# Regrouping a fused attention and FFN kernel, with weights and v cast in transfers that GpSimd issues

## The chip, the core and the metric

The kernel runs on one core of a Trainium2 chip. The core has TensorE (PE, with its own row PEld for weight loads), VectorE (DVE), ScalarE (ACT), GpSimd (POOL) and SyncE (SP), which work through queues of their own and wait for each other by semaphores; 16 DMA engines move data between HBM and SBUF. The metric is the device time of one execution in microseconds. Before the change the median of three runs was 226.99 us (226.62 to 227.18).

## The reference

Two layers follow each other. The first is a decayed linear attention over 4 batches, 8 heads, 768 positions of 64 elements, in blocks; the second is a bilinear FFN over the 3072 tokens that result.

```
for each block of 64 positions, per batch and head:
    intra = ((qb @ kb.T) * Dmask) @ vb          # Dmask[i,j] = lam**(i-j) for i >= j
    inter = (qb * lam**(pos+1)) @ kv_state
    out   = intra + inter
    kv_state = lam**64 * kv_state + (kb * lam**(63-pos)).T @ vb
x = out, heads side by side: 3072 x 512
y = ((x @ w_a) * (x @ w_b)) @ w_out             # w_a, w_b: 512 x 1536, w_out: 1536 x 512
```

Inputs and output are float32.

## The kernel before

A unit is 128 positions of one batch with all eight heads, so there are 24 units, six to a batch. Units are gathered into groups, and a group passes through the FFN together: `GROUPS` on line 28 is (4, 1, 2, 4, 4, 4, 4, 1). The first four units are packed and treated by code of their own (from line 868), because their q and k come in by eight transfers laid out for them.

**Attention of a unit, in pieces.** `prep_k` scales k and q by powers of lam into one bf16 tile (`make_ks`, `make_qs`, line 401) and, for units in `DMA_T`, issues a DMA transpose on SP; other units are transposed on PE (`piece_T`, `tps`, line 443, with a copy on ACT). `prep_v` casts v from float32 to bf16 on the engine that `VB_ENG` names (`make_vb`, lines 418 and 420). `piece_S` does the scores (`kq`, line 457) and the causal mask: either DVE multiplies PSUM by the triangle `lotri` (line 480) or ACT copies the scores to SBUF first (line 471) and DVE multiplies there (line 472). `piece_V` updates the running state `kvd` in PSUM and copies it to SBUF as `st` (lines 527, 558, 560). `pieces_O` makes the outputs of a pair of units (`o_ps`, line 497), whose evacuation (`evac_o`, lines 520 and 522) writes `xT`, the transposed input of the FFN.

**The FFN in three forms.** `ffn` is the plain form: per slice of 128 columns of d_ff, four matmuls for `a_ps`, four for `b_ps` (line 596), a copy of a on ACT (line 605), a product on DVE (line 623) into `ab`, and later output matmuls `op` (line 643). `ffn_z` replaces the eight block products of a 2 x 2 block matrix product by seven, for w_a and w_b: sums of weight blocks `wz_a`, `wz_b` (`weight_sum`) and of blocks of `xT` (`z_add`, `z_sub`, `z_mix` in `x_sums`, lines 705 to 707) are made beforehand; the partial products go through the PSUM banks U, V and W (line 730), copies of intermediate states on ACT (`snap`, line 811), subtractions on DVE (`oab`, lines 759 to 776) and a product on DVE (`ab`, line 738). The output step `op` has a seven-product form too: `ab_sum` makes sums of `ab` blocks (`zab`, lines 825 to 831), `out_sum` sums of w_out (`wy`, line 290), and `out_half` does half of one of the seven products (line 852). `Z_GROUPS` names the groups that use seven products in the first step (3 to 6), `ZO_GROUPS` those that use them in the output step (4 to 6); group 3 ends in `out_plain` (line 792), groups 0, 1, 2 and 7 are plain in both. A four-unit group needs 168 matmuls of 256 columns in the first step in seven-product form, and 84 of 256 columns in the output step, where the plain output step needs 48 of 512.

**Order.** The order of the work is written out by hand. `PLAN` lists for each group what is to be issued at which slot of its FFN: pieces of attention for coming groups, output halves of the group before (`H`), sums (`SM`, `WS`, `WO`, `X`), casts (`C`). `hook(slot)` issues them at that place, and each engine then takes its instructions in that order, waiting only for their inputs and buffers. Where output halves of the group before stand between the first-step products of a group, the code calls the group joined.

**Loads.** All loads of q, k, v and the weights are issued by SP as plain transfers of float32 (`load_x`, line 187; `load_w`, lines 221 and 228). Weights go into staging slots borrowed from other tiles and are cast to bf16 by DVE, ACT or POOL (`cast_w`, lines 240 to 254); `pump` issues the next pending load when a slot is free or when a unit has come close enough (`LOOKAHEAD`). The output is stored by SP, the very last part by ACT.

Of the kernel before, what the change touches and what calls it, by code (L numbers as in the profile page):

```python
# [22 lines left out]
def _bc(ap, dims):  # L23
# [4 lines left out]
GROUPS = (4, 1, 2, 4, 4, 4, 4, 1)  # L28
# [3 lines left out]
LOOKAHEAD = {9: 2, 10: 1}  # L32
DMA_T = range(7, 24)
KEEP_GROUPS = 2
PACK = 4

PLAN = {
# [38 lines left out]
}  # L81
Z_GROUPS = (3, 4, 5, 6)
ZO_GROUPS = (4, 5, 6)
FIN_AT = 5
N_LATE = 3
EV_ENG = {(u, b): "act" for u in range(24) for b in range(2)}
# [992 lines left out]
```

## Time and profile before

| | |
|---|---|
| median of three runs | 226.99 us |
| span of the profiled execution | 224.66 us (224.7 on the page) |
| granted TensorE clock | 1.000 |
| PE, DVE, ACT, POOL busy | 214.6, 164.8, 123.2, 101.1 us |
| HBM read, written | 28.32 MB, 6.29 MB |
| first matmul of the FFN | 18.16 us |
| first seven-product matmul | 84.74 us |
| last matmul group starts | 218.92 us |

The profiled execution has no other time than its span beside it: the time of the runs also holds what lies around the first and last instruction, and median and span are 2.33 us apart. Busy spans of one engine can overlap by some tens of nanoseconds, so counts times mean durations give more than the busy time, and for PE the distance between the starts of neighbouring rows says what an instruction costs. A line such as L596 is one line of the kernel, and several uses can share it. The window view gives, for each stretch, busy microseconds and the number of instructions of each engine, the granted clock, the mean busy share of the DMA engines and the GB/s that they moved.

### The profile page before, as it was taken

The page shows a single profiled execution, that of the slowest core. Times are in us where ns is not written, and L with a number is a line of the kernel's source. Part 1 is how long each engine was busy: PE and PEld are TensorE (multiplying, and loading weights), DVE is VectorE, ACT ScalarE, POOL GpSimd, SP SyncE. Part 2 cuts the span into 40 slices and gives each one's busy share as a digit, 9 for nine tenths or more (in the row PEclk, how much of TensorE's full clock was granted, in tenths as well). Part 3 has the DMA queues.
Part 4 walks back from the last instruction along what each step waited for, and adds up shares of the span by engine and source line. Part 5 has one row for each costly group of instructions (what it writes and reads, how often), then busy time and mean ns, then how long its engine had stood idle before and what let it go on. Part 6 is the DMA issues. An engine that isn't in the chain of part 4 may idle for free.

```text
span 224.7 us, 5609 instructions
## 1 busy us (share of the span) xinstructions
PE 214.6 (96%) x2235; PEld 158.8 (71%) x2235; DVE 164.8 (73%) x269; ACT 123.2 (55%) x251; POOL 101.1 (45%) x95
## 2 busy tenths in 40 slices
PE   7699999989989999999999999899999999999994
PEld 2375444437768757887547878688888888887994
DVE  1895673599699659989878999968686765777440
ACT  3586446017544247775366988776536665533322
POOL 6061004256895075541459359786417722052000
PEclk9999999999999999999999999999999999999999
DMA  4999999998999999999999999652021100112042
GB/s 137 316 231 356 356 384 346 276 217 192 229 198 218 219 180 240 204 253 247 175 240 243 243 206 202 138 98 48 2 88 55 50 1 4 47 48 95 0 143 93
DMA packets 99081, 39.42 MB, mean 175 GB/s; under 512 B 85488, under 2 KB 95088, under 8 KB 99056
## 3 DMA queue, kind: packets, MB, share of 16 engines
q1 hardware_dynamic: 98768, 39.00, 78.0%
q8 instruction: 17, 0.28, 0.5%
q10 hardware_dynamic: 288, 0.07, 0.1%
q14 instruction: 8, 0.07, 0.1%
HBM read 28.32 MB, written 6.29 MB: 154 GB/s over the span
## 4 chain that ended last, share of the span: by engine, by line
PE 80%; DVE 6%; DMA 6%; ACT 3%; issue 2%; SPq 1%; ACTq 0%; DVEq 0%
PE U L730 17%; PE op L852 12%; PE b_ps L596 9%; PE op L643 8%; PE V L730 8%; PE a_ps L596 8%; PE op L792 5%; PE W L730 4%; DMA wst<-in_moe_w_b_dram 4%; PE o_ps L497 3%; DMA k<-in_k_dram 3%; PE kq L457 2%; PE kvd L527 1%; SPq L350 1%; DVE m L480 1%
## 5 line engine op out<-in xcount | busy, mean ns | idle before, releaser
L811 ACT COPY u<-U 128x512 f32<-128x512 f32 x48 | 28.4, 591 | 16.9 <-PE U L730 16.6
L401 POOL TENSOR_TENSOR qk<-kf,lp_k 128x512 bf16<-128x512 f32 x18 | 19.8, 1099 | 34.6 <-DMA kf<-in_k_dram 23.1
L623 DVE TENSOR_TENSOR ab<-a_sb,b_ps 128x128 bf16<-128x128 bf16 (+2 forms) x48 | 19.2, 417 | 14.0 <-ACT a_sb L605 11.1
L480 DVE TENSOR_TENSOR m<-kq,lotri 128x512 bf16<-128x512 f32 x40 | 25.7, 684 | 3.8 <-PE kq L457 3.6
L596 PE MATMUL a_ps<-xT,wa_sb 128*128 128x128 bf16 (+2 forms) x200 | 27.8, 268 | 0.6 <-ACT xT L520 0.5
L596 PE MATMUL b_ps<-xT,wb_sb 128*128 128x128 bf16 (+2 forms) x192 | 27.5, 272 | 0.7 <-ACT oab L736 0.5
L738 DVE TENSOR_TENSOR ab<-oab 128x1024 bf16<-128x1024 bf16 x24 | 18.4, 767 | 10.5 <-ACT oab L736 10.5
L401 POOL TENSOR_TENSOR qk<-qf,lp_q 128x512 bf16<-128x512 f32 x20 | 25.2, 1259 | 1.2 <-DMA qf<-in_q_dram 1.2
L605 ACT CAST a_sb<-a_ps 128x128 bf16<-128x128 f32 (+2 forms) x48 | 17.1, 375 | 14.4 <-PE a_ps L596 14.3
L643 PE MATMUL op<-wo_sb,ab 128*128 128x512 bf16 (+2 forms) x120 | 22.8, 337 | 0.2 <-DVE wo_sb L254 0.2
L596 PEld LDWEIGHTS <-wa_sb 128*128 128x128 bf16 x200 | 16.6, 98 | 6.6 <-issue 0.7
L596 PEld LDWEIGHTS <-wb_sb 128*128 128x128 bf16 x192 | 15.7, 98 | 7.3 <-DVE wb_sb L251 0.7
L730 PEld LDWEIGHTS <-wz_a 128*128 128x128 bf16 x192 | 18.2, 98 | 3.6 <-issue 0.7
L730 PEld LDWEIGHTS <-wz_b 128*128 128x128 bf16 x192 | 18.7, 98 | 2.2
L730 PE MATMUL U<-xT,wz_a 128*128 128x256 bf16 x96 | 18.3, 272 | 0.0
L730 PE MATMUL U<-xT,wz_b 128*128 128x256 bf16 x96 | 18.3, 272 | 0.0
L520 ACT CAST xT<-o_ps 128x512 bf16<-128x512 f32 (+1 forms) x24 | 12.2, 556 | 10.7 <-PE o_ps L497 10.5
L420 POOL CAST vb<-vf 128x512 bf16<-128x512 f32 x14 | 10.9, 778 | 13.9 <-DMA vf<-in_v_dram 13.9
L769 DVE TENSOR_TENSOR oab<-U,u 128x512 bf16<-128x512 f32 x24 | 16.4, 682 | 0.4 <-PE U L730 0.4
L730 PEld LDWEIGHTS <-wa_sb 128*128 128x128 bf16 x144 | 13.4, 97 | 4.5 <-issue 1.7
L643 PEld LDWEIGHTS <-ab 128*128 128x128 bf16 x120 | 10.1, 98 | 8.6 <-issue 0.3
L736 ACT CAST oab<-U 128x512 bf16<-128x512 f32 x24 | 14.2, 591 | 3.6 <-PE U L730 3.5
(126 smaller groups left out, 453.8 us busy)
## 6 DMA issues: line engine op xcount, KB each, us to landing
vf<-in_v_dram SPq DMA_DIRECT2D x24, 256.0 KB, 4.8
qf<-in_q_dram SPq DMA_DIRECT2D x20, 256.0 KB, 4.6
kf<-in_k_dram SPq DMA_DIRECT2D x20, 256.0 KB, 4.6
out_dram<-o_sb SPq DMA_DIRECT2D x18, 256.0 KB, 2.5
wst<-in_moe_w_a_dram SPq DMA_DIRECT2D x6, 512.0 KB, 8.5
wst<-in_moe_w_b_dram SPq DMA_DIRECT2D x6, 512.0 KB, 9.0
wst<-in_moe_w_out_dram SPq DMA_DIRECT2D x6, 512.0 KB, 10.6
out_dram<-o_kept SPq DMA_DIRECT2D x5, 256.0 KB, 4.4
```

The lines of the kernel that those rows point to most:

```text
L401: eng_of(eng).tensor_mul(dst.rearrange("p (c b) d -> p b c d", b=2), x[:].rearrange("p (b c) d -> p b c d", b=2), lp.rearrange("p (b c) o ...
L480: nc.vector.tensor_mul(m, kq[i], lotri_bc)
L596: nc.tensor.matmul(ps[:, lo:hi], lhsT=w_sb[:, s, f * 128:(f + 1) * 128], rhs=xT[:, s, lo:hi], start=(s == 0), stop=(s == KS - 1), skip_gro ...
L605: nc.scalar.copy(a_sb[:, :gt], ps[:, :gt])
L623: nc.vector.tensor_mul(ab[:, f, :gt], a_sb[:, :gt], ps[:, :gt])
L643: nc.tensor.matmul(op[:, lo:hi], lhsT=ab[:, f, t * 128:(t + 1) * 128], rhs=wo_sb[:, f, lo:hi], start=(f == 0), stop=(f == FC - 1))
L730: nc.tensor.matmul(ps[:, k, :], lhsT=wt[:, s, n * 128:(n + 1) * 128], rhs=rhs[i][:, s, :], start=(fresh and k == 0 and s == 0), stop=True, ...
L736: nc.scalar.copy(oab[:, 0], U)
L738: nc.vector.tensor_mul(ab[:].rearrange("p (h i) (t c) -> p h i t c", h=2, t=2)[:, :, n], o5[:, :, :, 0, :], o5[:, :, :, 1, :])
L769: nc.vector.tensor_sub(oab[:, 1], U, v1)
L811: nc.scalar.copy(t, ps)
L852: nc.tensor.matmul(ps[:, t, :], lhsT=lhs[p][:, n, t * 128:(t + 1) * 128], rhs=rhs[:, n, :], start=fresh, stop=True, skip_group_check=True)
```

## The change

`GROUPS` becomes (4, 2, 4, 4, 4, 4, 2). Group 0 and the two-unit group 1 are plain; groups 2 to 6 use seven products in both steps, the last one with blocks of 128 instead of 256 columns of `xT`. `out_plain` and the special end of the last plain group go away. v and the weights are loaded by transfers that GpSimd issues and that write bf16 straight into the tiles that the matmuls read (v into a pool of eight buffers), so the staging slots and all casts go away. Each such transfer has a place in `PLAN` (`L`), the first eleven entries a list of their own (`HEAD_L`), headed by a one-element copy on POOL that waits for the first chunk of k. SP keeps the loads of q and k; three of the pairs (units 4 to 6) are held by one-element memsets on DVE until their place in the plan. PE transposes the units 4 to 9, DMA the units 10 to 23. Masks are written into one tile for both halves, in place where ACT copies the scores; where ACT copies both, one DVE instruction of 1024 elements masks them. The whole plan and the tables that give work to engines are new.

```
-GROUPS = (4, 1, 2, 4, 4, 4, 4, 1)
+GROUPS = (4, 2, 4, 4, 4, 4, 2)
-DMA_T = range(7, 24)
+DMA_T = (10, 11, 12, 13, 14, 15, 16, 17, 18, 19, 20, 21, 22, 23)
+HEAD_L = (('gate', ('k', 0)), ('v', 0), ('v', 1), ('v', 2), ('v', 3), ('a', 0), ('a', 1), ('b', 0), ('b', 1),
+  ('a', 2), ('b', 2))
+N_VB = 8
 PLAN = {
     0: [
+        (2, 'L', ('a', 3)), (3, 'L', ('b', 3)), (5, 'L', ('a', 4)), (6, 'L', ('a', 5)), (7, 'L', ('b', 4)),
+        (9, 'L', ('b', 5)), (10, 'L', ('o', 0)), (11, 'L', ('qk', 4)), (12, 'L', ('o', 1)),
...
+JOINED = (3, 4, 5, 6)
-Z_GROUPS = (3, 4, 5, 6)
-ZO_GROUPS = (4, 5, 6)
+Z_GROUPS = (2, 3, 4, 5, 6)
...
+        if w == "v":
+            t = prep_pool.tile([128, H, D], BF16, name="vb", tag="vb", bufs=N_VB)
+            nc.gpsimd.dma_start(out=t, in_=vr[b, nb])
         else:
             t = ld_pool.tile([128, H, D], F32, name=w + "f", tag=w + "f")
+            if gate:
+                nc.vector.memset(t[0:1, 0, 0:1], 0.0)
+            nc.sync.dma_start(out=t, in_={"q": qr, "k": kr}[w][b, nb])
...
         if kind == "o":
+            nc.gpsimd.dma_start(out=wo_sb[:, 2 * c:2 * c + 2, :], in_=wo_r[:, 2 * c:2 * c + 2, :])
         else:
+            w, r = (wa_sb, wa_r) if kind == "a" else (wb_sb, wb_r)
+            nc.gpsimd.dma_start(out=w_part(w, c), in_=w_part(r, c))
...
+    def load(x):
+        kind, i = x
+        if kind == "gate":
+            nc.gpsimd.tensor_copy(tiny, x4[i[0], i[1]][0:1, 0, 0, 0:1])
+        elif kind == "qk":
+            for w in "kq":
+                load_x(w, i, True)
+        elif kind == "v":
+            load_x("v", i)
+        else:
+            load_w(kind, i)
...
+    def mask(kq, n_act=0):
+        m = msk_pool.tile([128, H, 128], BF16, name="m", tag="m")
+        ms = [m[:, :HP], m[:, HP:]]
+        if n_act == 2:
+            for i in range(2):
+                nc.scalar.copy(ms[i], kq[i])
+            nc.vector.tensor_mul(m, m, lotri_all)
+            return ms
...
-        if g not in ZO_GROUPS:
-            out_plain(u0, ab, hook)
-        elif own:
+        if own:
             fin.pop()()
-            for i in range(14):
-                hook(3 * NP + i)
+            for i in range(3 * NP, 3 * NP + 16):
+                hook(i)
```

More of the change, by code (lines that the diff above doesn't have):

```diff
@@ new lines @@
+Z_GROUPS = (2, 3, 4, 5, 6)
+KEEP = 4
+EV_ENG = {(4, 0): 'act',
+  (4, 1): 'dve',
+  (5, 1): 'dve',
+  (6, 0): 'act',
+  (6, 1): 'dve',
+  (8, 1): 'dve',
+  (10, 0): 'act',
+  (10, 1): 'dve',
+  (11, 0): 'act',
+  (12, 0): 'dve',
+  (14, 1): 'dve',
+  (15, 0): 'dve',
+  (15, 1): 'dve',
+  (19, 1): 'dve',
+  (22, 1): 'act'}
+MASK_ACT = {4: 1,
+  5: 0,
+  6: 2,
+  7: 1,
+  8: 0,
+  9: 2,
+  10: 1,
+  11: 0,
+  12: 1,
+  13: 1,
+  14: 2,
+  15: 1,
+  16: 0,
+  17: 1,
+  18: 0,
+  19: 1,
+  20: 1,
+  21: 0,
+  22: 1,
+  23: 0}
@@ new lines @@
+KV_ENG = {3: 'dve',
+  4: 'act',
+  5: 'act',
+  6: 'dve',
+  7: 'act',
+  8: 'act',
+  9: 'dve',
+  10: 'dve',
+  11: 'dve',
+  12: 'act',
+  13: 'act',
+  14: 'act',
+  15: 'act',
+  16: 'dve',
+  17: 'dve',
+  18: 'act',
+  19: 'act',
+  20: 'act',
+  21: 'act',
+  22: 'act',
+  23: 'act'}
+PQ_ENG = {4: 'pool',
+  5: 'pool',
+  6: 'pool',
+  7: 'pool',
+  8: 'dve',
+  9: 'pool',
+  10: 'pool',
+  11: 'dve',
+  13: 'pool',
+  14: 'dve',
+  15: 'pool',
+  17: 'pool',
+  20: 'pool',
+  21: 'pool',
+  22: 'pool',
+  23: 'dve'}
@@ new lines, in ffn, with ffn_plain @@
+        ops = [ps_bank("op", [128, d_model], F32, hold=True) for _ in range(n)]
+        for c in range(FC // 2):
+            for t in range(n):
+                out_mms(ops[t], ab, t, range(2 * c, 2 * c + 2))
+                if c == FC // 2 - 1:
+                    store(u0 + t, ops[t], 0, d_model)
+                hook(slot)
+                slot += 1
+        bank["held"].clear()
+    def ffn_plain(u0, n, xT, hook):
+        gt = n * BLK
+        ab = ab_pool.tile([128, FC, 512], BF16, name="ab", tag="ab")
@@ L870 @@
     xs4 = {"q": scr[0][:, 0:4, :], "k": scr[1][:, 0:4, :]}
+    for x in HEAD_L:
+        load(x)
     xT4 = {"q": scr[0][:, 4:8, :], "k": scr[1][:, 4:8, :]}
@@ L945 @@
     scale4("k", 1, 1)
-    for u in range(n0 - 1):
-        make_vb(u, "pool")
     scores4(0, (0, 1), ((5, 6), (0, 1)))
@@ L983 @@
     inter(3)
-    cast_w("a", 0, "first")
     evac_o((2, 3), 0)
```

478 lines of the change are left out of this document (189 added, 289 removed), and 90 rows, old and new, of the table PLAN.

## The prediction

> **What bounds the kernel now.** I read the page's busy shares first, then the windows by stage, then the timeline of the matmuls for their pitch and for the holes between them.
>
> ```profile
> PE 214.6 (96%) x2235; PEld 158.8 (71%) x2235; DVE 164.8 (73%) x269; ACT 123.2 (55%) x251; POOL 101.1 (45%) x95
> ```
>
> PE has work nearly always, so a microsecond is gained either by fewer matmul columns or by closing a hole. The timeline of PE gives both: when rows follow without a wait, the distance of their starts is the true price, because the busy spans overlap.
>
> ```profile
> 18.16 2.06 PE L596 MATMUL a_ps<-xT,wa_sb 128*128 128x256 bf16 x16
> 22.14 3.63 PE L596 MATMUL b_ps<-xT,wb_sb 128*128 128x512 bf16 x16 [0.20 <-DVE wb_sb L251]
> 29.06 1.89 PE L596 MATMUL a_ps<-xT,wa_sb 128*128 128x512 bf16 x8
> 30.79 1.89 PE L596 MATMUL b_ps<-xT,wb_sb 128*128 128x512 bf16 x8
> 45.94 0.40 PE L443 MATMUL tps<-ident,qk 128*128 128x128 bf16 x4 [0.73 <-DVE qk L401]
> 57.66 0.39 PE L596 MATMUL a_ps<-xT,wa_sb 128*128 128x128 bf16 x4
> 57.88 0.39 PE L596 MATMUL b_ps<-xT,wb_sb 128*128 128x128 bf16 x4
> 64.33 0.86 PE L596 MATMUL a_ps<-xT,wa_sb 128*128 128x256 bf16 x4 [0.46 <-ACT xT L520]
> 74.00 0.60 PE L596 MATMUL b_ps<-xT,wb_sb 128*128 128x256 bf16 x4
> 74.44 0.60 PE L596 MATMUL a_ps<-xT,wa_sb 128*128 128x256 bf16 x4
> 143.09 0.38 PE L730 MATMUL U<-z_sub,wa_sb 128*128 128x256 bf16 x2 [0.81 <-DVE oab L769]
> 204.62 0.38 PE L596 MATMUL b_ps<-xT,wb_sb 128*128 128x128 bf16 x4 [0.49 <-ACT oab L736]
> ```
>
> Pitches: 512 columns 1.73/8 = 0.216 us, 256 columns 0.44/4 = 0.109 (0.11 rounded up), 128 columns 0.22/4 = 0.056. Holes: a chunk of b weights arrives late (22.14), transposes wait for a scaled k (45.94), the two-unit group waits for xT (64.33), and DVE is behind in the seven-product stages (143.09).
>
> The windows say how near DVE is to being the bound there, and how fast weights arrive (columns: PE, PEld, DVE, ACT, POOL busy, clock, DMA share, GB/s):
>
> ```profile
> 11.20:16.80 5.60, 5.42 (x110) 4.28 (x109) 5.53 (x10) 4.80 (x11) 3.50 (x5) 1.00 0.93 230
> 22.40:33.70 11.30, 11.30 (x54) 5.12 (x53) 8.09 (x14) 5.41 (x9) 0.00 (x0) 1.00 1.07 370
> 85.00:105.00 20.00, 19.67 (x211) 16.41 (x209) 18.60 (x31) 14.30 (x27) 8.66 (x9) 1.00 1.26 239
> 119.00:143.00 24.00, 23.21 (x279) 18.63 (x277) 22.32 (x35) 19.97 (x40) 16.47 (x13) 1.00 1.06 204
> 143.00:172.00 29.00, 28.76 (x335) 24.26 (x335) 22.07 (x35) 18.38 (x38) 17.39 (x12) 1.00 0.33 77
> ```
>
> DVE is 93% busy in the first step of both four-unit groups without a neighbour's output step (85 to 105, 119 to 143), 76% where output products of the group before are mixed in. The granted clock is 1.00 throughout and plays no part.
>
> **The sum's base.** The profiled span is 224.66 us, the median 226.99; the terms below are taken off the span and the distance of 2.33 is kept.
>
> **1. Matmul columns.** From the two instruction orders: 512-wide output matmuls 132 to 72, -60 x 0.216 = -13.0; 256-wide output matmuls 264 to 378, +114 x 0.109 = +12.4; 128-wide ones in the FFN's first step 192 to 168 and in the last output 24 to none, against 24 more PE transposes (three units fewer are transposed by DMA): -24 x 0.056 = -1.3. Sum -1.9 us. Seven products instead of eight save only this, since three of the last five groups already had them; little here is open, for these are counts times pitches.
>
> **2. Weights and v.** Removed: 24 v loads and 18 weight loads from SP, their casts on DVE (6 v at 0.81, 12 weight pieces, 12 us in all), ACT (4 v at 0.63, 5 pieces, 7.3 us) and POOL (14 v at 0.78, 5 pieces, 15 us). Added: 42 transfers issued by POOL, the first behind a one-element copy that waits for the first k chunk, which had landed by 8.34 (its scaling started then). Every POOL instruction queues behind these issues: the q and k scalings and the sums.
> The trace has no transfer issued by POOL. SP's issues bound the price: 0.5 us each where free, 1.68 where the four v loads held it (6.71 us for four, from 5.28). I take 1.0, an estimate between them nearer the free rows, since the moment of blocking was one. The 16th issue (the last b chunk) then falls at 8.3 + 16 = 24.3. Data: at the 230 GB/s of the window in which v moved, 1 MB of v needs 4.6 us, from about 10 to 14.5; a 512 KB chunk at 370 GB/s 1.42 us. So the third chunk (first of b) lands near 18.8 and the twelfth near 31.5. PE wants them at 21.4 and 35.2 (its present starts less the gain here). Both hold. Gain: the a stage of 16 x 0.109 + 8 x 0.216 = 3.5 us ended at 22.14 instead of 21.6, -0.5; the first a weights passed casts on POOL and DVE for which PE's weight loads waited 0.4, -0.3; the third v's cast on POOL ended near 15.1, when the state matmuls that use it began, -0.2. I take -1.0; ends -1.5 (some of the waits for k gone too) and, at 1.68 an issue, +2 (last issue 35.2, landing some 2 us after).
> SP keeps the q and k loads, the stores and fourteen DMA transposes instead of seventeen; these no longer stand behind 42 other entries, some of which held the queue for over 4 us (a k load at 31.85). I book nothing for it, since PE's holes name no load of q or k after 11 us. The loads of units 4 to 6 now wait for one-element memsets on DVE, six at no more than the 0.27 of the only memset row; the casts that leave the window 22 to 34 (8.09 of 11.3 busy) cover them, and without that cover they are 1.6 us of DVE.
> Later v loads must wait for one of eight buffers; POOL then holds scalings behind them. 42 issues are 42 us on POOL, whose arithmetic falls from 101 to about 77 (14 k scalings x 1.10, 16 q x 1.26, the sums at 1.64, three weight sums x 3.09): 119 of 222 us, so no bound.
>
> [...]
>
> **3. Holes between 40 and 86 us.** At 44.82 to 46.54 eight transposes (0.45 us of work) took 1.7, 1.3 lost; 63.2 to 65.0 lost 0.9 (evacuation of xT, then the a copy); 85.4 to 86.1 lost 0.5 (z_add). The new order puts 24 output matmuls ahead of the first transposes and six (1.3 us) plus eight transposes between the evacuation and the next FFN group; z sums have 18 output matmuls (3.9 us) as cover, and need 0.7 + 1.3. The k scaling that came late was behind a cast, two weight sums and the state copy on DVE. I take -2.5; ends -2.7 and -1.3, since unit 5's q scaling now follows a 3.09 us weight sum, another scaling and a v issue on POOL, which leaves under a microsecond.
>
> **4. The seven-product stages.** DVE gains 12 us (by means: 24 small `ab` -6.8, casts -12.3, and +18 narrow and 6 narrow `oab`/`ab` about 10, `xT` 6 x 0.68, scalings 8 x 0.69, sums and `o_sb` 11, z sums 2.9; 0.92 of it is net, as busy 164.8 is of the 179 that counts times means give), so 177 of 222. What matters is the third group: PE has 168 x 0.109 = 18.4 plus 3.2 of attention, 21.6; DVE has 18 `oab` x 0.684, 5 `ab` x 0.767, eight mask pieces 5.8, state, scalings, xT 4.0, in all 26.0, net 24. That is over PE by 2.4; before the ratio was 0.93. A lag of about a microsecond fits into the banks: +1.5. The next group: DVE 30.3, PE 31: +0.3. Against it the holes of 143.09 (1.0) and at 121 and 132 (0.4) are in groups that now have 28 against 31: -1.2. Sum +0.6; ends -1.4 and +3.
>
> **5. The last group.** Two units at half width. Per pair PE has 28 x 0.056 = 1.6 us, ACT four copies of 0.37, DVE four of about 0.42; with fourteen output halves of the group before between them this fits. The last pair has none: copy, subtraction and copy on one bank, then copy 0.37, product 0.42, sums before the output products, one on POOL at about 0.8. I count 1.2 of waits against the 0.7 that goes at 204.62: +0.5; ends -0.5 and +2.5. The end: the last copy is 0.37 instead of 0.27 and 128 KB land in 1.7 instead of 1.6: +0.2.
>
> Sum: -1.9 - 1.0 - 2.5 + 0.6 + 0.5 + 0.2 = -4.1, a span of 220.6 and a time of **222.9 us**.
>
> **Rivals.** A: the casting transfers run slower than plain ones, or their issue starves. Place: the first group's weights. At the 230 GB/s that short v rows had, a chunk takes 2.28 us, and the twelfth lands at 14.5 + 27.4 = 41.9 against 35.2: 6.7 late. Without term 2 the rest is -3.1, so 230.6. It decides from a chunk time of (35.2 + 3.1 - 14.5)/12 = 2.0 us, 265 GB/s. For it: v's rate, and no row of such a transfer; against it: the present 370 leaves 3.7 us of slack. [...]
> B: DVE becomes the bound. The third and fourth group need 54.3 of DVE; if no more than 0.95 of the time can be filled, 57.2 against PE's 52.6, +4.6 instead of +0.6 net: 226.9. For it: 22.32 of 24 at 119 to 143, with holes; against it: at 85 to 105 the same ratio cost 0.8.
> C: nearly every hole goes: term 4 at -1.0, term 5 at -0.5, term 2 at -1.5: 220.3 or below.
>
> **Chances.** Forecast 0.50 (221.3 to 225.5), C 0.17, B 0.13, A 0.15, other mishaps 0.05. What a measurement can tell from no change is about 0.3%, 0.7 us. Faster: 0.50 + 0.17 + 0.05 of B = 0.72; same 0.04 (B); slower 0.24. The range of 219.0 to 229.0 leaves out most of A and the best of C.
>
> **What would show it.** Right: b_ps starts before 21.7 and the last b step before 35.5 without a DMA wait; no wait at the first transposes; DVE over 23 us in the third group with PE holes of 1 to 2 us; some 1 us of PE waits in the last pair. Wrong: PE waiting for weights from the transfers, POOL issues far over 1 us with scalings late behind them, or PE losing over 3 us to DVE.

## The result, and the profile after

The changed kernel took 248.47 us (248.11 to 248.74, four runs), the kernel before 227.09 beside it: 1.094 times as long, 95% interval 1.091 to 1.097. The prediction was 222.9 in a range of 219.0 to 229.0, so it was wrong in sign and far out of range. The profiled execution of the changed kernel took 248.11, with a span of 246.4.

The page of the changed kernel, busy time and share of each engine, and the granted clock in 40 slices:

```profile
PE 218.8 (89%) x2262; PEld 164.1 (67%) x2269; DVE 178.4 (72%) x290; ACT 124.7 (51%) x250; POOL 108.8 (44%) x112
...
PEclk9999999959999999997999999999999999999999
```

PE is busy 89% of the span instead of 96%, and the clock, at full speed throughout before, now falls in some slices. DVE and POOL are no busier in share than before (72 and 44% against 73 and 45%). So the loss is in waits of PE. The waits of PE, summed by what ended them (engine, line waited for, total, times, longest):

```profile
PE tps L528 <- POOL qk L498: 4.0, 1, 4.0
PE kq L542 <- DMA qkT<-qk: 3.5, 3, 1.7
PE U L809 <- DVE oab L847: 2.7, 1, 2.7
PE op L907 <- DVE zab L884: 2.4, 1, 2.4
PE b_ps L678 <- DVE ab L705: 1.8, 2, 1.6
```

Before, PE waited 0.8 us for `oab` and 0.7 for a k that DVE scaled, the longest of its waits once the first group ran; of the others above it had none. The timeline of PE gives their places (start, length, and in brackets the wait in front):

```profile
18.86 3.65 PE L678 MATMUL a_ps<-xT,wa_sb 128*128 128x256 bf16 x23 [1.10 <-DMA wa_sb<-in_moe_w_a_dram]
22.34 1.89 PE L678 MATMUL b_ps<-xT,wb_sb 128*128 128x512 bf16 x8
...
50.65 1.04 PE L528 MATMUL tps<-ident,qk 128*128 128x128 bf16 x8 [4.03 <-POOL qk L498]
...
71.59 0.60 PE L678 MATMUL b_ps<-xT,wb_sb 128*128 128x256 bf16 x4 [1.61 <-DVE ab L705]
...
110.58 0.58 PE L809 MATMUL U<-z_sub,wa_sb 128*128 128x256 bf16 x2 [2.74 <-DVE oab L847]
...
135.45 0.40 PE L542 MATMUL kq<-qkT 64*128 64x128 bf16 x8 [1.44 <-DMA qkT<-qk]
...
165.47 0.72 PE L907 MATMUL op<-wo_sb,zab 128*128 128x256 bf16 x5 [2.37 <-DVE zab L884]
...
170.44 0.40 PE L542 MATMUL kq<-qkT 64*128 64x128 bf16 x8 [1.74 <-DMA qkT<-qk]
```

The first a step waits 1.1 us for a chunk of weights, but the first b step starts at 22.34, 0.2 later than before, and the last at 36.15 without a wait: the weights are not what costs. The first large hole stands in front of the transposes of unit 5, which before (at 54.98) had no wait in front. The windows that answer to those of the prediction, with two after holes (columns: PE, PEld, DVE, ACT, POOL busy, clock, DMA share, GB/s):

```profile
22.40:33.70 11.30, 11.25 (x53) 5.10 (x53) 5.51 (x12) 2.93 (x5) 7.48 (x8) 1.00 1.31 202
50.00:54.00 4.00, 3.35 (x14) 1.59 (x14) 0.00 (x0) 1.01 (x1) 4.00 (x3) 0.50 1.08 192
85.00:105.00 20.00, 19.67 (x247) 16.07 (x245) 18.48 (x31) 14.73 (x30) 5.73 (x5) 1.00 0.89 146
110.00:114.00 4.00, 3.42 (x18) 2.39 (x18) 3.97 (x7) 0.94 (x2) 0.35 (x1) 0.58 1.01 205
119.00:143.00 24.00, 22.34 (x268) 18.76 (x267) 19.95 (x32) 12.71 (x26) 11.33 (x11) 1.00 1.09 155
143.00:172.00 29.00, 24.31 (x259) 19.84 (x258) 25.08 (x35) 15.46 (x32) 10.88 (x9) 1.00 0.67 121
```

From 85 to 105 the seven-product step runs as before (PE 19.67 of 20, DVE 18.48 where it had 18.60). In 143 to 172 PE loses 4.7 us of 29. Behind the holes at 46 and 107 the clock is 0.50 from 48.5 to 55.3 and from 110.0 to 113.4.

To place the loss I add up the holes of PE: the distance from one row of matmuls to the next less the row's own pitch (0.216, 0.109 and 0.056 us for 512, 256 and 128 columns), so that matmuls at a lower clock count as holes too.

| stretch of the span, us | holes before | holes after | difference |
|---|---|---|---|
| 0 to 40 | 7.3 | 7.9 | +0.6 |
| 40 to 80 | 3.3 | 11.4 | +8.1 |
| 80 to 100 | 1.2 | 1.5 | +0.3 |
| 100 to 170 | 3.6 | 13.9 | +10.3 |
| 170 to the end | 1.1 | 6.2 | +5.1 |

That is +24.4; with the matmul columns saved (-1.9) and an end that is 0.9 longer it makes +23.4 for a span that is 21.7 longer. The rest of 1.7 is the error of this sum; a few records of matmuls are missing from the trace (the page has 2262 matmuls beside 2269 weight loads; before, 2235 of both).

### The profile page after: what moved, and what is told of

Its sections match the earlier page's. It is cut to its first block, busy times and chain, and to the rows that moved or that the text cites. A ratio compares the mean times of both kernels' runs of the same rounds, so it can differ in the third digit from the quotient of the medians.

```text
span 246.4 us, 5649 instructions
## 1 busy us (share of the span) xinstructions
PE 218.8 (89%) x2262; PEld 164.1 (67%) x2269; DVE 178.4 (72%) x290; ACT 124.7 (51%) x250; POOL 108.8 (44%) x112
## 3 DMA queue, kind: packets, MB, share of 16 engines
q0 software_dynamic: 31904, 7.87, 32.9%
## 4 chain that ended last, share of the span: by engine, by line
PE 58%; DMA 16%; DVE 9%; issue 8%; POOL 3%; ACT 3%; SPq 1%; DVEq 0%; ACTq 0%; POOLq 0%
PE op L907 14%; PE U L809 13%; PE V L809 9%; DMA qkT<-qk 6%; DMA qf<-in_q_dram 5%; PE W L809 4%; PE b_ps L678 4%; PE a_ps L678 4%; PE o_ps L579 4%; DMA wa_sb<-in_moe_w_a_dram 3%; PE op L725 3%; PE kq L542 2%; DMA k<-in_k_dram 2%; POOL vb L322 2%; POOL qk L498 1%
## 5 line engine op out<-in xcount | busy, mean ns | idle before, releaser
L863 ACT COPY u<-U 128x512 f32<-128x512 f32 (+1 forms) x60 | 32.9, 548 | 30.0 <-PE U L809 29.6
L817 DVE TENSOR_TENSOR ab<-oab 128x1024 bf16<-128x1024 bf16 (+1 forms) x30 | 25.4, 848 | 15.0 <-ACT oab L815 14.8
L498 POOL TENSOR_TENSOR qk<-kf,lp_k 128x512 bf16<-128x512 f32 x14 | 15.8, 1126 | 33.8 <-DMA kf<-in_k_dram 18.5
L809 PEld LDWEIGHTS <-wz_b 128*128 128x128 bf16 x240 | 22.4, 98 | 2.2
L322 POOL DMA_DIRECT2D vb<-in_v_dram x24 | 22.2, 926 | 1.0 <-DMA wb_sb<-in_moe_w_b_dram 1.0
L907 PE MATMUL op<-wy,ab 128*128 128x256 bf16 x162 | 22.5, 278 | 0.0
L809 PE MATMUL U<-xT,wz_a 128*128 128x256 bf16 (+1 forms) x120 | 21.6, 262 | 0.0
L809 PE MATMUL U<-xT,wz_b 128*128 128x256 bf16 (+1 forms) x120 | 21.6, 262 | 0.0
L863 ACT COPY u<-V 128x512 f32<-128x512 f32 (+1 forms) x30 | 16.4, 548 | 8.2 <-PE V L809 7.8
L678 PE MATMUL b_ps<-xT,wb_sb 128*128 128x512 bf16 (+1 forms) x95 | 18.2, 325 | 1.8 <-DVE ab L705 1.8
L678 PE MATMUL a_ps<-xT,wa_sb 128*128 128x256 bf16 (+1 forms) x103 | 18.2, 313 | 1.1 <-DMA wa_sb<-in_moe_w_a_dram 1.1
L847 DVE TENSOR_TENSOR oab<-U,u 128x512 bf16<-128x512 f32 (+1 forms) x30 | 18.8, 627 | 0.0
```

Of the source, the lines that this page charges most:

```text
L322: nc.gpsimd.dma_start(out=t, in_=vr[b, nb])
L498: eng_of(eng).tensor_mul(dst.rearrange("p (c b) d -> p b c d", b=2), x[:].rearrange("p (b c) d -> p b c d", b=2), lp.rearrange("p (b c) o ...
L678: nc.tensor.matmul(ps[:, lo:hi], lhsT=w_sb[:, s, f * 128:(f + 1) * 128], rhs=xT[:, s, lo:hi], start=(s == 0), stop=(s == KS - 1), skip_gro ...
L809: nc.tensor.matmul(ps[:, k, :], lhsT=wt[:, s, n * 128:(n + 1) * 128], rhs=rhs[i][:, s, :], start=(fresh and k == 0 and s == 0), stop=True, ...
L817: eng_of(MU_ENG.get((g, n), "dve")).tensor_mul(ab[:].rearrange("p (h i) x -> p h i x", h=2)[:, :, n, :2 * hw] .rearrange("p h (t c) -> p h ...
L847: nc.vector.tensor_sub(oab[:, 1], U, v1)
```

## Is a casting transfer slow?

In the changed kernel's trace the weights seem to come at half the rate: 202 GB/s from 22.4 to 33.7, 370 before. The first theory was therefore that casting transfers are slow. It was put to the test by itself: the same four chunks, back to back, plain from SP, casting from POOL, plain from POOL.

```
phase(nc.sync, F32, A, W, "w_sp")
phase(nc.gpsimd, BF16, B, W, "w_cast")
phase(nc.gpsimd, F32, A, W, "w_pool")
```

> Computes nothing of the reference: eleven phases of four transfers back to back, each phase behind a wait for the one before; the output is filler. Two warm-up phases, then weight chunks of 512 KB, 256 columns by 4 rows per partition (plain on SP's queue, casting on GpSimd's, plain on GpSimd's), the same three for the 512 KB chunks of the out-weights (2 rows of 2 KB per partition), the same three for v (256 KB in 256-byte rows). Theory 1, the casting transfer is itself slow: the casting phases move their bytes at 180 to 220 GB/s (2.4 to 2.9 us per 512 KB chunk, four in about 10.5), the plain ones at 330 to 380 (1.4 us each, four in about 5.7), whoever issues them. Theory 2, the issuer is what is slow (GpSimd's queue): plain transfers from GpSimd are as slow as the casting ones. [...]

The timeline: issue of four transfers, then DVE's read of the last one that landed.

```profile
19.24 2.02 SPq L33 DMA_DIRECT2D w_sp<-in_moe_w_a_dram  x4
27.85 0.34 DVE L40 COPY acc<-w_sp 128x1 f32<-128x1 f32 x4 [8.64 <-DMA w_sp<-in_moe_w_a_dram]
28.48 2.97 POOL L33 DMA_DIRECT2D w_cast<-in_moe_w_b_dram  x4 [15.38 <-DVE acc L40]
37.18 0.34 DVE L40 CAST acc<-w_cast 128x1 f32<-128x1 bf16 x4 [8.99 <-DMA w_cast<-in_moe_w_b_dram]
37.81 3.00 POOL L33 DMA_DIRECT2D w_pool<-in_moe_w_a_dram  x4 [6.36 <-DVE acc L40]
46.74 0.34 DVE L40 COPY acc<-w_pool 128x1 f32<-128x1 f32 x4 [9.22 <-DMA w_pool<-in_moe_w_a_dram]
```

From first issue to last landing 8.6, 8.7 and 8.9 us for weights; 8.4, 7.8 and 9.1 for out-weights; 6.6, 6.9 and 7.4 for v. Neither the cast nor the issuer made four transfers more than 0.8 us slower, so theories 1 and 2 fell; the 5.7 us expected for four plain chunks was missed as well, by all three alike. The view of GB/s counts what is written: the page of the changed kernel has 7.87 MB for POOL's queue, half of the 15.73 MB of float32 that its 42 loads read. So 202 GB/s beside a DMA share of 1.31 stands for some 400 read, an estimate, which is about the old rate of 370.

## One part undone, one part alone

Three kernels undo parts of the change: v, the weights, or both go back to plain loads from SP with staging and casts.

```
-            nc.gpsimd.dma_start(out=t, in_=vr[b, nb])        # a_w0, a_00
+            nc.sync.dma_start(out=t, in_=vr[b, nb])          # and make_vb as before
...
-            nc.gpsimd.dma_start(out=w_part(w, c), in_=w_part(r, c))   # a_0v, a_00
+            nc.sync.dma_start(out=t, in_=w_part(r, c))                # and cast_w as before
```

> The changed kernel's groups, products and plan of work, with weights and v loaded by plain transfers from SP and cast by VectorE, ScalarE and GpSimd as before. Theory 1 (slow casting transfers): the losses before 60 us go away, in all 223 to 231 us. Rival, the new grouping and plan themselves lose the time (VectorE becomes the bound, transposes and loads late whoever moves v): 240 us or more.

> The changed kernel with v alone put back to plain loads and casts; the weights still come by casting transfers. Theory 1: the weights are three quarters of the cast bytes before 60 us, so most of the loss stays: 238 to 247 us, with the first slices' rate still near 190 GB/s. If it is v's issues on GpSimd that cost (its engine stretched beside VectorE at 105 to 108 us and the late transposes): 230 to 236.

> The changed kernel with the weights alone put back to plain loads, staging and casts; v still comes by casting transfers. Theory 1: 228 to 235 us, with the first weight chunks landing as in the kernel before (near 370 GB/s) and only the losses after 60 us left. If v's issues are what costs: 240 or more. If the regrouping is: 240 or more here too, and in the run with both put back.

Measured: 255.4 with both undone (1.124, 1.115 to 1.132), 251.1 with v undone (1.105, 1.098 to 1.112), 264.0 with the weights undone (1.161, 1.154 to 1.169), where PE waits 12 us before 28 us for the first v's, again beside weights in another queue. No undoing helps, so the plan of groups loses time whoever moves the data. The kernel with both undone has a hole of 12.3 us at 45, where out-weights wait for a cast that stands badly in this plan; that is an artefact of the mixture. Without it some 243 would be left, an estimate. The two kernels with v undone lack the waits at 107 and 162 us: compared with the changed kernel they gain 2.8 to 3.1 and 2.5 to 2.6 us there.

Then the reverse: the kernel before, with its groups and plan, and only the transfers of the change.

```
+HEAD_L = (('gate', ('k', 0)), ('v', 0), ..., ('v', 3), ('a', 0), ('a', 1), ('b', 0), ('b', 1), ('a', 2), ('b', 2))
+LOADS = ((0, ('a', 3)), (1, ('b', 3)), (2, ('a', 4)), ..., (5, ('qk', 4)), ..., (8, ('v', 4)), ...)
-            nc.sync.dma_start(out=t, in_=w_part(r, c))                # b_wv, b_w
+            nc.gpsimd.dma_start(out=w_part(w, c), in_=w_part(r, c))
...
+            nc.gpsimd.dma_start(out=t, in_=vr[b, nb])                 # b_wv, b_v
```

> The kernel before with its groups and plan kept, and only weights and v brought by casting transfers that GpSimd issues (no staging, no casts, loads of units 4 to 6 held back by the same markers as in the changed kernel). After the transfers measured alone (8.6, 8.7 and 8.9 us for the same four weight chunks, plain, casting, and plain from GpSimd), slow casting is no longer a theory. If the transfers were harmless and the regrouped plan carries the loss: 224 to 229 us. If the transfers lose time inside the kernel, by GpSimd's issues stretching VectorE or by two queues sharing the 16 engines: 232 us or more.

> The kernel before with only the weights brought by GpSimd's casting transfers; v by plain loads and casts as before. With both, the time was 232.6, 6 us over before, with new holes at 16 us (1.5, GpSimd's half of a mask), at 20 to 24 (1.3 more than before, a late weight chunk), at 100 (1.8) and at 123 (1.5). If the two early holes are the weights' doing (GpSimd's queue of issues and its order behind v) and the two late ones v's: 229 to 231 us here, the late holes gone. If the weights carry all of it: 232 to 234.

> The kernel before with only v brought by GpSimd's casting transfers. If v's issues in GpSimd's later runs cost the holes at 100 and 123 us: 229 to 231 us, those holes still there. If v is harmless: 225 to 228 us, faster than or equal to the kernel before, with 24 casts gone from VectorE, ScalarE and GpSimd. The loads of the first four v's on a second queue may also come late, as in the changed kernel with only v cast (holes of 12 us before 28 us): then 235 or more.

Measured: both 232.64 (1.025, 1.017 to 1.032), the weights alone 239.4 (1.055, 1.045 to 1.066), v alone 253.9 (1.119, 1.111 to 1.127). So the transfers cost 6.0 us in a plan that was not made for them, where I had booked a gain of 1.0, and groups and plan cost the other 15.8; taken off in the other order the shares would differ, since no undoing in the new plan gave those 6.0 back. The waits of PE with both:

```profile
PE U L705 <- ACT u L786: 1.8, 1, 1.8
PE V L705 <- DVE z_sub L680: 1.5, 1, 1.5
PE o_ps L472 <- POOL m L453: 1.5, 1, 1.5
```

The third is POOL's half of a mask behind its own issues; behind it the clock is 0.50 from 19.7 to 23.1, and the first a step takes 5.15 us where it took 3.98. Each half alone is worse than both, which I had not expected: the early holes are larger there, because v and the weights then stand in two queues. With v alone on POOL's queue beside weights on SP's:

```profile
PE kv L546 <- DMA vb<-in_v_dram: 8.1, 2, 4.6
PE kvd L546 <- DMA vb<-in_v_dram: 4.0, 1, 4.0
...
DMA to landing us min/median/max: 9.7/15.2/17.8
```

The first four v's land 9.7 to 17.8 us after their issue (4.3 alone, in the run below). In the mirror image (weights on POOL's queue, v on SP's) it is v on SP's that lands late (6.5 to 12.8 us after their issue, for those before 40 us), and POOL's casts of it cost PE 4.3 and 1.4 us.

## Two queues beside each other

```
phase("sp_big", nc.sync, nc.gpsimd, F32, BIG, B, V[1])      # v on SP, eight out-weight chunks on POOL
phase("pool_big", nc.gpsimd, nc.sync, F32, BIG, B, V[2])    # v on POOL, the chunks on SP
phase("sp_small", nc.sync, nc.gpsimd, F32, SMALL, S, V[0])  # beside eight of 384 KB in 256-byte rows
```

> Computes nothing of the reference; the output is filler. Six phases apart from each other: four v transfers (256 KB each in 256-byte rows) alone on SP; on SP beside eight out-weight chunks (512 KB, 2 KB rows) on GpSimd's queue; on GpSimd's queue beside eight such chunks on SP's; on SP beside eight transfers of 384 KB in 256-byte rows on GpSimd's; on SP beside eight casting out-weight chunks; and on SP's own queue with eight out-weight chunks behind them. Theory of rows (the queues take turns row by row, so that small rows get a ninth of the bytes beside 2 KB rows): the last v lands some 6 us after its phase begins when alone, 11 to 15 us beside large rows on either queue, 8 to 10 beside small rows, 6 to 8 in one queue. Theory of bytes (each queue gets half of the rate while both have work): 7 to 9 us beside large rows and small rows alike.

Issue to landing of four v transfers, one line for each phase: alone; on SP beside large rows; on POOL beside SP's large rows; on SP beside small rows; in one queue ahead of large rows.

```profile
DMA to landing us min/median/max: 3.4/4.3/4.7
DMA to landing us min/median/max: 3.1/10.4/15.8
DMA to landing us min/median/max: 6.7/8.2/9.3
DMA to landing us min/median/max: 3.2/8.1/19.5
DMA to landing us min/median/max: 3.2/4.4/4.8
```

From the first issue of v to DVE's read of the last v it is 6.8 us alone, 17.8 on SP beside POOL's queue, 12.1 on POOL beside SP's, 21.7 beside small rows, 6.9 in one queue; beside eight casting chunks on POOL's queue, the sixth phase, it is 18.7. Both theories fell: beside small rows it is no better than beside large ones, and it is no equal share of the bytes either.

The packets show the difference. While both queues have work (the phase with large rows, 16 to 22 us; POOL's queue, then SP's: packets as the profile counts them, MB, share of the engines' time):

```profile
q0 software_dynamic: 566, 2.06, 93.7%
q1 hardware_dynamic: 566, 0.14, 11.6%
```

Each queue moved 566 packets, but POOL's held 3.6 KB each and SP's 256 bytes, one row of v. So in these 6 us SP's v moved one fifteenth as many bytes. Small rows did not help, because POOL's packets hold several of them: from 56 to 66 us 587 packets of 3.5 KB stand beside 431 of SP's. Beside large rows, then, the counts are equal (566 and 566), and beside small ones SP's queue moved 0.73 times as many packets as POOL's. In the changed kernel, from 36 to 48 us:

```profile
q0 software_dynamic: 3625, 1.17, 84.5%
q1 hardware_dynamic: 3685, 0.93, 58.3%
```

Again the counts are nearly equal (3625 and 3685), and SP's loads of q and k get 0.93 MB in 12 us, 78 GB/s, where the four v's alone, with rows of the same size, moved at 234 (3 to 7 us of the measurement).

## The loads before 60 us, and the clock

Unit 5's q in the changed kernel: POOL waits for it, scales it, and the transposes follow.

```profile
35.43 3.64 SPq L327 DMA_DIRECT2D qf<-in_q_dram  x1
49.55 1.04 POOL L498 TENSOR_TENSOR qk<-qf,lp_q 128x512 bf16<-128x512 f32 x1 [4.34 <-DMA qf<-in_q_dram]
```

Issued at 35.4, it landed at 49.5. In the kernel before the same scaling started at 47.61, with its load issued at 40.88, but unit 5 was then in the third group and due later; with two units in the second group PE wants it at 46.5. Three kernels: its loads issued earlier, fewer bytes beside them, and the hole filled.

```
# e_order
+(6, 'L', ('qk', 4)), (8, 'L', ('qk', 5)), (14, 'L', ('qk', 6))     # were slots 11, 14, 21
# e_halfw
-(17, 'L', ('o', 3)), (18, 'L', ('o', 4)), (20, 'L', ('o', 5))
+nc.gpsimd.memset(wo_sb[:, FC // 2:], 0.0)
# e_warm, in piece_T
+        for _ in range(70 if u == 5 else 0):
+            nc.tensor.transpose(tps[:, 0, 0, :], U[4]["qk"][:, 0, 0:2, :], ident)
```

> The changed kernel with the loads of q and k of units 4, 5 and 6 issued at slots 6, 8 and 14 of the first group instead of 11, 14 and 21, ahead of most out-weight chunks. If q of unit 5 comes late (49.5 us) because its load stands behind the out-weights and v in the shared engines: it lands before 44, the hole of 4.2 us at 46 closes, the clock does not fall after it (the further 3 us to 59 go), in all 240 to 243 us. If the weights then come late instead, the hole moves to the first FFN step: 246 us or more.

> The changed kernel without the loads of the last three out-weight chunks (1.5 MB of source, issued by GpSimd at 30 to 36 us); that half of the out-weights is zero, so the output is not the reference's. Theory: between 17 and 50 us the 16 engines are full (share 1.35 to 1.5), and the loads of q and k on SP's queue get what GpSimd's queue leaves, so 1.5 MB less brings q of unit 5 some 4 us earlier (45 instead of 49.5): the hole of 4.2 us at 46 shrinks below 1, the clock does not fall after it, 239 to 243 us. If q and k are held back by something else (their markers, SP's own issuing, the small rows): the hole stays over 3 us, 246 to 249.

> The changed kernel with 70 idle transposes (of unit 4's data, into the bank that unit 5's transposes then overwrite; some 3.9 us) put on TensorE in the hole at 46 us. If the clock of 0.50 from 48 to 55 us comes from the idle time and not from what TensorE does after: the clock stays at 1.0 there, the first product of the third group comes about 3 us earlier (82 instead of 85.2 us), in all 245 to 246 us. If it does not depend on the hole, or the loads set the pace up to 85 us whatever the clock: 85 us as before, 248 to 249.

Issued earlier: 248.16 us, no gain. The issues themselves take longer (6.2 us for unit 5's k, 4.2 for its q), q lands at 48, and the hole is still 2.9. With 1.5 MB less on POOL's queue, and an output that is not the reference's: 245.14 (1.081, 1.071 to 1.090). POOL's wait for unit 5's q, and PE's:

```profile
45.26 1.38 POOL L498 TENSOR_TENSOR qk<-qf,lp_q 128x512 bf16<-128x512 f32 x1 [1.52 <-DMA qf<-in_q_dram]
```

```profile
PE tps L528 <- POOL qk L498: 1.1, 1, 1.1
```

It comes at 45.3 instead of 49.5, PE waits 1.1 instead of 4.0, the clock stays at 1.00, and the first product of the third group starts 5.9 us earlier (78.7 instead of 84.6). Shown, then: what makes unit 5 late is POOL's transfers in the shared engines, not the moment of its own issue. Only 3.3 of the 5.9 us are left at the end; a hole at 128 (2.2, then a clock of 0.50) is new, and that it took the rest is read from the trace.

The filled hole shows the clock by itself: from 48 to 56 us it is 1.00 instead of 0.63, 0.50 and 0.67, and the third group starts 2.1 us earlier (1.1 from its second pair on). In the changed kernel's trace the clock stays at 0.50 for 3.41 us or twice that when it falls (6.83 us from 48.51, 3.41 from 109.95), and PE had not been idle for such a stretch before: it was busy for 1.52 of the 3.41 us before the fall at 48.51. Nor does the length of a wait decide: that of 2.7 us at 107, and that of 2.2 at 128 in e_halfw, were followed by 0.50, and the one of 2.4 us at 163 was not. What tells the waits apart in the changed kernel's trace is where they lie. The two falls are 18.0 steps of 3.413 us apart. Counted in such steps from the first fall, both ways, the clock was at 0.50 after the three steps in which PE was busy for 1.52 us or less (1.52 and 1.28 in the two from 45.10 on, 1.30 before the fall at 109.95) and at 1.00 after every other one between 4.1 and 243.1 us, in which it was busy for 1.67 or more (1.95 in the step around the wait at 163, which two steps share). The time was 251.4 (249.85 in the profiled execution), and unit 17's transposed q and k then came 3.3 us late at 133. What is won before 85 us does not last by itself.

## GpSimd's runs and the late transposes

The hole at 163 us in the changed kernel: POOL's rows and DVE's.

```profile
159.39 0.94 POOL L322 DMA_DIRECT2D vb<-in_v_dram  x1
160.34 1.05 POOL L498 TENSOR_TENSOR qk<-kf,lp_k 128x512 bf16<-128x512 f32 x1
161.35 1.04 POOL L498 TENSOR_TENSOR qk<-qf,lp_q 128x512 bf16<-128x512 f32 x1
162.35 1.03 POOL L498 TENSOR_TENSOR qk<-kf,lp_k 128x512 bf16<-128x512 f32 x1
163.35 1.03 POOL L498 TENSOR_TENSOR qk<-qf,lp_q 128x512 bf16<-128x512 f32 x1
```

```profile
159.67 5.27 DVE L817 TENSOR_TENSOR ab<-oab 128x1024 bf16<-128x1024 bf16 x1 [0.63 <-ACT oab L815]
```

POOL issues a v load and scales two units without a pause until 164.38. DVE's product, usually 0.68 us, begins inside that run and ends at 164.94, 0.56 us after the run's end. The same holds at 105.93 (2.80 us, ending 0.57 after POOL's scaling) and at 68.17 (2.44, also 0.57). PE's holes at 110, 165 and 71 stand behind these three. All three are operations with both operands in SBUF; those of 512 columns with an operand in PSUM take 0.67 to 0.69 us in the whole trace. DVE's whole stretched time (over the shortest instruction of the same kind) is some 15 us against 11 before, so the sum changed little: before, no single operation took over 2.3 us, and PE's longest wait for DVE in the seven-product stages was 0.8.

Not every run of POOL holds DVE so long. At 116.84 DVE's mask also met two POOL instructions in a row:

```profile
115.61 1.64 POOL L882 TENSOR_TENSOR zab<-ab 128x768 bf16<-128x768 bf16 x1
117.22 1.49 POOL L498 TENSOR_TENSOR qk<-kf,lp_k 128x512 bf16<-128x512 f32 x1
```

```profile
116.84 0.97 DVE L556 TENSOR_TENSOR m<-m,lotri 128x1024 bf16<-128x1024 bf16 x1 [0.56 <-ACT m L555]
```

It ended 0.55 us after the first of them, and the second took 1.49 us instead of 1.04. The difference stands in front of the run: the scalings at 67.99, 106.11 and 160.34 follow a v issue within 0.02 us, the sum at 115.61 does not. The traces of all the kernels agree. A DVE operation waited through several POOL instructions 31 times, each time in a run that began within 0.02 us of an issue; in runs without an issue directly in front DVE got in after one instruction, all 124 times that it had to wait (of issues farther in front, the nearest ended 0.10 us ahead); and one run behind an issue (at 70.7 in a_0v) let it in as well. No kernel was made to try this alone.

First three smaller repairs:

```
# e_port
-MASK_ACT 6: 2        +MASK_ACT 6: 0
-PQ_ENG 14: 'dve'     +PQ_ENG 14: 'pool'
-(8, 'P', 22)         +(11, 'P', 22)                       # of plan 4, ahead of ('SM', (4, 0))
# e_look
-LOOKAHEAD = {9: 2, 10: 1, 16: 1, 17: 2, 18: 2, 4: 3, 7: 1, 19: 1}
+LOOKAHEAD = {9: 2, 10: 1}
# e_break
-PQ_ENG 14: 'dve'     +PQ_ENG 14: 'pool'
-(8, 'P', 22)         +(12, 'P', 22)                       # behind ('SM', (4, 0)), which POOL must wait for
```

> The changed kernel with three placements altered so that no VectorE operation with both operands in SBUF falls into an unbroken run of GpSimd work at the three places where one was stretched: the mask of unit 6 taken straight from PSUM (two operations instead of ScalarE's copies and one of 1024 columns), the scaling of unit 14's q on GpSimd instead of VectorE, and unit 22's scalings three slots later. If such an operation waits until GpSimd's run ends (2.44, 2.80 and 5.27 us where 0.68 is usual), the holes of 1.6, 2.7 and 2.4 us behind them close: 239 to 243 us. If VectorE's total load is what bounds these stages, the holes only move: 245 to 248.

> The changed kernel with the look-ahead of the q and k loads as in the kernel before (entries for units 4, 7, 16, 17, 18 and 19 dropped). If the late transposes at 133.6 and 168.3 us (waits of 1.4 and 1.7 us) come from loads that were let go too late: these waits go, 243 to 246 us. If they come from GpSimd's four scalings in a row, no change: 246 to 249.

> The changed kernel with two of GpSimd's runs changed: unit 14's q scaled by GpSimd instead of VectorE, and unit 22's scalings placed behind GpSimd's own block sum of the fifth group, which cannot start before VectorE and TensorE have come that far (moved by slots alone they still ran in one piece with unit 21's). Theory: VectorE's operation with both operands in SBUF ends 0.55 us after the end of GpSimd's run whatever the run's length; with the run at 159 us cut from 5.0 to 3.0 us it takes 3.2 instead of 5.27 us and the hole behind it falls from 2.4 to about 0.4; the one at 107 from 2.7 to 1.6 as already seen. Time 243 to 246 us if nothing takes their place; 247 to 250 if the next wait in line does.

Measured: 250.8, 249.6 and 250.1 us (248.3 to 251.8 the last), none better than the changed kernel. Locally the theory held. With unit 14's q on POOL the wait at 107 fell from 2.74 to 1.58. The new slot alone moved nothing, because POOL does not follow PE's slots: the run and the 5.27 us came again. Behind a sum for which POOL has to wait, the run was three instructions long, and the product took what was expected (3.2):

```profile
162.74 3.28 DVE L817 TENSOR_TENSOR ab<-oab 128x1024 bf16<-128x1024 bf16 x1 [0.63 <-ACT oab L815]
```

The wait behind it went. But the mask taken from PSUM only let the next operation with SBUF operands be the one that waits (2.96 us, PE 2.3), and in e_break the waits for transposed q and k at 134 and 168 grew to 2.2 and 2.1, each now followed by a clock of 0.5 to 0.6. With the longer look-ahead (e_look) these fell to 0.85 and 0.55, but a hole of 1.5 at 121 was new and the wait for unit 5 at 46 was 5.2 us.

So the repairs together, v undone in part, and the sum with fewer bytes:

```
# e_late
-LOOKAHEAD = {9: 2, 10: 1, 16: 1, ...}    +LOOKAHEAD = {9: 2, 10: 1}
-PQ_ENG 14: 'dve'                         +PQ_ENG 14: 'pool'
-(7, 'P', 21), (8, 'P', 22)               +(3, 'P', 21), (12, 'P', 22)
# e_sum: e_late and e_halfw;  e_vlate: v of units 4 to 23 as before the change;  e_both: e_late and e_vlate
```

> The changed kernel with four placements mended together: look-ahead of the loads as in the kernel before, unit 14's q scaled by GpSimd, unit 21 scaled three slots earlier (ahead of GpSimd's block sums of the fourth group), unit 22 behind GpSimd's block sum of the fifth group. Theory: the waits after 85 us are one chain (load, scaling, transposing transfer of 4.3 us, scores) beside GpSimd's runs, so only mended together do they give: the holes at 107 (2.7), 134 (1.4), 162 (2.4) and 168 us (1.7) fall below 1.6, 0.9, 0.5 and 0.5, 241 to 245 us. If another bound lies right behind (VectorE's total work in the groups of 85 to 170 us), 247 to 250.

> The changed kernel with v of units 4 to 23 put back to plain loads on SP and casts; v of units 0 to 3 and all weights still come by GpSimd's casting transfers. Theory: without v's issue GpSimd's runs at 105 and 159 us are a fifth to a third shorter and start at other times; the holes of 2.7 and 2.4 us behind VectorE's stretched operations go, as they did in the run with all of v put back. Against it stand 20 casts on GpSimd, VectorE and ScalarE. 241 to 246 us; if v's issues are not the cause, 248 to 252.

> The same four placements, and without the loads of the last three out-weight chunks (that half of the out-weights is zero, so the output is not the reference's). If the losses before 60 and after 85 us are separate and add up: 235 to 240 us. If what is won before 85 us is given back after, as 2 us were in the run without those loads alone: 241 to 245.

> The changed kernel with v of units 4 to 23 by plain loads and casts again, and with the four mended placements. Each alone gave 5.7 us, but both close the holes at 107 and 162 us; only the gain before 85 us (2.5, from v) and the late transposes (some 2.5, from the placements) are separate. 238 to 241 us if the rest is bound by the loads before 60 us and the clock; 236 or less if the repairs add up in full.

| kernel | us | ratio to before, interval |
|---|---|---|
| four placements mended (e_late) | 242.83 | 1.070, 1.065 to 1.074 |
| later v by plain loads (e_vlate) | 242.78 | 1.069, 1.061 to 1.078 |
| both (e_both) | 242.17 | 1.071, 1.066 to 1.077 |
| placements mended and 1.5 MB less (e_sum) | 236.69 | 1.043, 1.039 to 1.046 |

Mended together the placements give 5.6 us, as expected, where the smaller repairs gave nothing. The earlier place of unit 21, which also takes its scalings out from behind the issue of a v, is new here and was not run alone; so it may be that place, and not the joint repair, that made the difference. The waits of PE with placements mended and 1.5 MB less:

```profile
PE kq L542 <- DVE m L563: 1.8, 2, 1.1
...
PE U L809 <- DVE oab L847: 1.6, 1, 1.6
...
PE tps L528 <- POOL qk L498: 1.1, 1, 1.1
...
PE kq L542 <- DMA qkT<-qk: 0.8, 1, 0.8
```

Each of the five large waits is now under 2 us and the clock is 1.00 up to 234 us. The gain of 11.8 is 2.9 more than the two parts' 5.6 and 3.3 (each known to 1 or 2 us), and the trace gives the reason: the hole at 128 that took back what the loads won is gone. Of the two kernels with v's later loads undone, the first shows that taking these loads off POOL's queue is worth as much as the placements (DVE then never waits through several POOL instructions, but fewer bytes also stand beside q and k), the second that the two do not add up: e_both was expected at 238 to 241 and came at 242.2, with a hole of 1.9 at 69 followed by a clock of 0.5, and new ones of 1.2 at 98 and 1.4 at 150. Why it ends where its two parts end is not settled.

## Why the prediction was wrong

**Matmul columns, -1.9.** Held: the pitches are the same, 0.216 and 0.109, and the counts are those of the code. It is the only gain that came.

**Weights and v, -1.0.** The prices were about right: a weight issue takes POOL 0.70 to 0.84 us and a v issue 0.88 to 1.07 (forecast 1.0), the a stage ends as before, and rival A's slow transfers do not exist (8.7 us against 8.6). The step that failed is "I book nothing for it, since PE's holes name no load of q or k after 11 us": it leaves out a gain for caution and does not ask whether these loads can lose. A view of waits names what is late now, not what becomes late. From 36 to 48 us SP's queue moved about as many packets as POOL's (3685 and 3625), its rows of 256 bytes came at 78 GB/s, single transfers took 10 us and more instead of 4.3, and this was not in the sum at all. In the old plan the transfers cost 6.0 us (b_wv) instead of gaining 1.0.

**Holes between 40 and 86, -2.5.** Failed, and most plainly: +8.1 from 40 to 80. The step says that unit 5's q scaling "leaves under a microsecond" after POOL's other work. It looked at POOL's queue and not at the landing of the load that it scales: the trace of before has that scaling at 47.61, and the new order's transposes come at 46.5. With 1.0 for the scaling that subtraction shows a wait of up to 2 us even without POOL's transfers, less what the earlier issue of the load (35.4 instead of 40.9) wins. With them q landed at 49.5; the low clock behind the hole took more.

**Seven-product stages, +0.6.** Failed: +10.3 from 100 to 170. I weighed DVE's total against PE's, and the total was no reason: from 85 to 117 DVE is busy 28.9 of 32 us, before 28.2, so rival B is not what happened. What counts is single operations that wait for a whole run of POOL work behind a v issue (2.80 and 5.27 us), and transposed q and k that come late because a look-ahead of one unit puts load, scaling and transfer in a row. The sum counted DVE's work by busy time and had no term for waits of DVE: in 124 cases of all the traces an operation waited through one POOL instruction, and directly behind an issue through up to four scalings in a row (5.27 us).

**Last group, +0.5, and the end, +0.2.** Too small: +5.1 of holes from 170 on, of which the wait in front of 170.44 is 1.7 and belongs to the late transposes; the end is 0.9. The rest is many waits of 0.2 to 0.5 us for ACT and DVE at half width. No run took these apart; even the best one has 5.4 us of holes there.

**Clock.** "Plays no part" was true of the kernel before only. From 48.5 to 55.3 and from 110.0 to 113.4 it is 0.50, and by estimate some 4 of these 10.2 us go to it.

Of the 21.4 us the runs thus show: about 3.3 for the transfers of the last three out-weight chunks in the way of q and k, 5.6 for the placements, some 3 more for both being cured at once. That leaves 9.6 between the kernel that has all this, and leaves out three chunks, and the one before; the 6.0 that the transfers cost in the old plan may be part of it. That the last group has some 4 of the 9.6 and the remaining holes around 100 us some 3 is read from the trace, not tested. No kernel that was run beats the one before.

## What to carry to other kernels

Before a load goes to another queue or a group is made larger, take from the trace when each later input lands and subtract when the new order wants it: waits that are hidden now are no evidence. Keep transfers in one queue in the order of need, or count packets: in m2_queues two queues moved 566 each in 6 us, and four transfers in packets of 256 bytes took 17.8 and 21.7 us beside the other queue instead of 6.8. Where POOL must issue a load, do not let its arithmetic follow within 0.02 us beside DVE's SBUF operations; that is read from the traces and not tried. In a full schedule one repair hands its gain to the next wait, so find the whole chain (load, scaling, transpose, and POOL's runs beside DVE's SBUF operations) and try the repairs together before judging any.

## What the runs showed of the hardware

- Casting during the transfer took 8.7 us against 8.6 for 2 MB in four weight chunks, 7.8 against 8.4 for out-weights, 6.9 against 6.6 for four v's. The view of GB/s counts written bytes: 7.87 MB for loads that read 15.73.
- Four transfers of 256 KB took 6.8 us alone and 17.8 beside eight chunks on POOL's queue, 21.7 beside 256-byte rows there, 12.1 when the queues were swapped, 6.9 when all stood in one queue. Beside the eight chunks both queues moved 566 packets in 6 us, of 256 bytes on SP's and 3.6 KB on POOL's. SP's issues of such loads stretched too, from a median of 0.74 us alone to 6.2 in e_order.
- A DVE operation with both operands in SBUF that met a run of POOL instructions begun within 0.02 us of a load issue ended 0.56 us after the run: 5.27 and, with the run shortened, 3.28 us instead of 0.68. Without the issue directly in front it got in after one instruction (0.97 us). A v issue behind the last scaling (at 69.99) did not hold it.
- In the changed kernel PE's clock fell to 0.50 for 6.83 us at 48.51 and for 3.41 at 109.95, 18.0 steps of 3.413 us apart. Counted in such steps it was at 0.50 after those in which PE was busy for 1.52, 1.28 and 1.30 us, and at 1.00 after all others, with 1.67 or more; the wait of 2.7 us at 107 lowered it, the one of 2.4 at 163 did not.
